# AV moved into 64x64 tiles around the scores of a later block, relu's input in two PSUM banks, and a new table of priorities

## The chip, the cores and the metric

The kernel runs on one core of a Trainium2 chip. The metric is the device time of one execution in microseconds (us). Five engines work in parallel, each with its own instruction order fixed when the program is built: TensorE (PE, with its weight loads as PEld), VectorE (DVE), ScalarE (ACT), GpSimd (POOL) and SyncE (SP), which here only issues DMAs. They wait for each other by semaphores.

## The reference

Attention within a window of 32 positions to both sides, over 8 batches, 8 heads, 576 positions and 64 channels, followed by two matrix products with a squared relu between them:

```python
scores = np.matmul(q, k.transpose(0, 1, 3, 2)) / np.sqrt(64)
scores = np.where(np.abs(pos[:, None] - pos[None, :]) <= 32, scores, -1e9)
attn = np.exp(scores - np.max(scores, axis=-1, keepdims=True))
attn = attn / (np.sum(attn, axis=-1, keepdims=True) + 1e-09)
x = np.matmul(attn, v)          # to 4608 tokens x 512
r = np.maximum(x @ w_in, 0.0)   # 512 x 2048
out = (s * (r * r) + b) @ w_out # 2048 x 512
```

Inputs and output are float32; the products run in bfloat16.

## The kernel before

The 4608 tokens are cut into 36 blocks of 128. Block `j` goes through these steps:

- SP loads q, k and v of the block (three DMAs of 256 KB, L456; in two pieces where a block crosses a batch). POOL, and early ACT and DVE, cast them to bf16 (`kqn`, `ve`, and `vo`, which is v shifted by half a block). `turned` and `lastload` keep the loads in one order on SP.
- q and k are transposed into `kqt`: by PE up to block 8, from there by one DMA transpose of 256 KB on SP (`k_turn`, L539).
- `scores` (L596): 16 matmuls on 64x64 quarters of the PE array into the two `SC` banks. Where the ring of `kqt` buffers wraps, a part of them is split and there are 24.
- DVE adds the mask and takes the maximum (L605), ACT takes the exponential with its sum (L612), DVE inverts the sum (L620, L623), POOL multiplies (L477). The result `p` is transposed into `pts`: by PE for blocks 0 to 3, then by a DMA transpose of 256 KB on SP (L639).
- `av` (L667): 16 matmuls of 128 rows by 64 columns of weights each (the page writes 128*64), into one bank `AV`. DVE casts this to `XT` (L476, the group `xt<-av`).

The rest is the feed-forward part (FFN), in 8 tiles of 128 tokens and then 14 of 256. `s1` (L758): `XT` times `w_in`, 16 matmuls of 128 columns or 8 of 256, into a PSUM bank: `HT[0]`, `HT[1]` and, from token 1024 on, also `TPF` (shown as `tp`). ACT takes the relu of the bank (L767), DVE squares it (L786). `s2` (L809): 16 matmuls of 512 columns, in steps of four, into `OUTP` or `PTPF` (shown as `ptp`), in the last three tiles also into `SC[1]` and `AV`. DVE scales and adds (L818, `outs`), SP stores 256 KB (L823). Where the plan expects PE to be idle early on, `fill` (L408) puts matmuls of no use into the order.

The order on every engine comes from a planner, `_Plan.order`. It walks through time with a cost for each step, and on each engine takes the ready step with the least `key`: about the token number, an offset for the kind of the step, and `RANK`, a shift by kind (two rows: blocks 0 to 11, and the others). For PE it adds 95 ns (`SWITCH`) when the mode of tiling changes (full array, 128*64, 64*64). For a DMA it keeps a time at which the DMA engines are free, and adds `dtime`. The order is then fixed; on the chip an engine that meets a wait stops, and what stands behind it on that engine stops too.

Of the kernel before, what the change touches and what calls it, by code (L numbers as in the profile page):

```python
# [24 lines left out]
PE_SLACK, STEADY = 400.0, 60000.0  # L25
SWITCH, STICK, STAY = 95.0, 1500, 60000.0
BIAS = {"act": 0.0, "dve": 400.0, "pool": 0.0}
FILL, FILL_MIN, FILL_SHARE, FILL_NS, WARM = ("attn", "ffn", "sums"), 300.0, 0.7, 115.0, 9000.0
# [34 lines left out]
class _Plan:  # L63
# [10 lines left out]
    def add(self, eng, fn, cost, key, reads=(), writes=(), dsem=None, ndma=1, dtime=0.0,  # L74
            after=(), behind=None, ndesc=128):
        n = _Node(len(self.nodes), eng, fn, cost, 300.0 if eng == "pe" else 130.0, key, dsem,
                  ndma, dtime)
        n.ndesc = ndesc

        def dep(m, raw):  # L80
            if m is not None and m is not n:
                n.deps[m] = bool(n.deps.get(m)) or raw

        for m in after:
            dep(m, True)
        if behind is not None:
            assert behind.eng == eng
            n.deps[behind] = None
        for r in reads:
            dep(self.writers.get(r), True)  # L90
        for w in writes:
            dep(self.writers.get(w), True)
            for m in self.readers.get(w, ()):
                dep(m, False)
        for r in reads:
            self.readers.setdefault(r, []).append(n)
        for w in writes:
            self.writers[w] = n
            self.readers[w] = []
        self.nodes.append(n)  # L100
        return n

    def order(self):
# [29 lines left out]
        while len(out) < len(self.nodes):  # L133
# [29 lines left out]
            if e == "pe" and n.mode != mode:  # L163
                free[e], mode = free[e] + SWITCH, n.mode
            if n.dsem is None:
                end = free[e] + n.lat
            else:
                early = t < STEADY
                if e == "sp" and early:
                    free[e] = room(free[e], n.ndesc)  # L170
                dma_free[e] = max(dma_free[e], free[e] + (ISSUE if early else 1300.0)) + n.dtime
                if e == "sp" and early:
                    dma_free[e] += TURN if (n.ndesc == 512) != (kind == 512) else 0.0
                    kind = n.ndesc
                end = dma_free[e] + (LAND if early else 700.0)
                if e == "sp":
                    queue.append((dma_free[e], n.dtime, n.ndesc))
                    del queue[:-12]
            for u in n.users:
                if u.deps[n] is None:  # L180
                    u.ready = max(u.ready, free[e])
                else:
                    late = PE_SLACK if u.eng == "pe" and t > STEADY else 0.0
                    u.ready = max(u.ready,
                                  end + late if u.eng != n.eng or n.dsem else free[e] + 60.0)
                u.left -= 1
                if u.left == 0:
                    offer(u)
# [70 lines left out]
    stage = None  # L259


def bass_sliding_window_symmetric__then__act_starrelu_kernel(
# [15 lines left out]
    LEAD, L0, LS = 640, 300, 50  # L278
# [13 lines left out]
    RANK = ({"ptc": 200, "ou": 120, "no": -20, "av": -120, "vo": 0, "ktc": 0, "ck": 200, "rc": -160, "cv": 20, "ktd": 320, "cq": 400, "wo": 340, "s1": -240, "kt": -60, "wi": -40, "xt": -280, "re": 80, "pt": -40}, {"vo": 40, "pt": -60, "ex": -200, "ck": -320, "s2": -80, "av": 580, "qt": -320, "mx": 320, "s1": -20, "sc": 40, "kt": 80})  # L292
    EARLY = 12

    def rank(kind, j):
        return RANK[0 if j < EARLY else 1].get(kind, 0)

# [10 lines left out]
    def OSET(j):  # L308
        return ("act", "dve")
# [3 lines left out]
    with ExitStack() as es:  # L313
# [45 lines left out]
        PTPF = ps((128, 512), F32, "ptp")  # L359
        AV = ps((128, NPAIR, 128), F32, "av")  # L360
# [91 lines left out]
        def load(src, t0, dst, name, key, sem, x):  # L452
            pcs = parts(t0)

            def fn(e):
                return [e.dma_start(dst[r:r + n, :].rearrange("p (h d) -> p h d", h=H),  # L456
                                    src[b, :, s0:s0 + n, :].rearrange("h s d -> s h d"))
                        for (b, s0, r, n) in pcs]

            tot = sum(n for (_, _, _, n) in pcs)  # L460
            gate = turned.get(x - GATE)
            lastload[0] = add("sp", fn, 640.0 * len(pcs), key, writes=[name], dsem=sem,
                              ndma=len(pcs), dtime=1150.0 * tot / 128, behind=lastload[0], ndesc=8 * tot,
                              after=[gate] if gate and gate.eng == "pe" else [])
            if gate and gate.eng == "sp":
                lastload[0].deps.setdefault(gate, None)

        def cast(engs, src, sname, dst, dname, key, costs=None):
            move(engs, costs or {"act": 620.0, "dve": 425.0, "pool": 640.0}, dst, src, key,
                 sname if isinstance(sname, list) else [sname], [dname])  # L470
# [46 lines left out]
        def make_vo(j):  # L517
# [9 lines left out]
            for r0, x in ((64, j), (0, j + 1)):  # L527
                sl = x % (NL + 1)
                move(OSET(j), {"act": 620.0, "dve": 425.0},
                     VO[s_][r0:r0 + 64, :], V32[sl][r0:r0 + 64, :],  # L530
                     akey(j) - 10 + rank("vo", j), [("V32", sl)] + ([("V32", 0, "lo")] if x == 0 else []),
                     [("VO", s_, r0)])


        def k_turn(j):
            kn, kt = j % NB, j % NKT
            key = akey(j) - 128
            if j > KQDMA:
                add("sp", lambda e: [e.dma_start_transpose(KQT[kt][:, :, :], KQN[kn][:, :])],  # L539
                    1300, key + 64 + rank("ktd", j), reads=[("KN", kn), ("QN", kn)],  # L540
                    writes=[("KT", kt), ("QT", kt)], dsem=f"dkt{kt}", dtime=1600, ndesc=1024)
                return
# [7 lines left out]
            move(FLEX(j - 1), {"dve": 430.0, "act": 620.0}, KQT[kt][:, 0:NPAIR, :], TP[:, 0:4, :],  # L550
                 key + rank("ktc", j), ["TP"], [("KT", kt)])

        def q_turn(j):
# [12 lines left out]
            move(FLEX(j), {"dve": 430.0, "act": 620.0}, KQT[qt][:, NPAIR:2 * NPAIR, :], TP[:, 4:8, :],  # L566
                 key + rank("qtc", j), ["TP"], [("QT", qt)])

        def attend(j):
# [7 lines left out]
            def half(blk, pr, a):  # L577
                return ((NKT - 1 - blk) * 2 * NPAIR + pr) * 2 + a

            def scores(e):  # L580
# [19 lines left out]
            add("pe", scores, 215, key + rank("sc", j), reads=[("KT", ka), ("KT", kb), ("QT", kb)],  # L600
                writes=[("SC", 0), ("SC", 1)]).mode = 2
            for y in range(8):
# [12 lines left out]
                    390, key + 2 + rank("ex", j), reads=[("SS", ss, x), ("MX", mb, y)],  # L615
                    writes=[("P", pb, y), ("SM", mb, y)])
            fine = j < FINE
            for c0, c1 in ((0, 4), (4, 8)) if fine else ((0, 8),):
# [5 lines left out]
                    180, key + 3 + rank("rc", j), reads=[("SE", mb, c0)] + [("SM", mb, y) for y in ys],  # L624
# [7 lines left out]
            for part, (c0, c1) in enumerate(((0, 4), (4, 8)) if fine else ((0, 8),)):  # L632
# [5 lines left out]
                if j >= PDMA:  # L638
# [3 lines left out]
                        writes=[("PTS", ptb, y) for y in range(8)], dsem=f"dpt{ptb}", dtime=1600, ndesc=1024)  # L642
                else:
                    def turn(e, c0=c0, c1=c1, ptp=ptp):
                        for y in range(c0, c1):
# [6 lines left out]
                         {"act": 190.0 + 0.83 * 128 * (c1 - c0), "dve": 50 + 95.0 * (c1 - c0)},  # L652
                         PTS[ptb][:, c0:c1, :], ptp[:, c0:c1, :], key + 4 + rank("ptc", j), [pres],
                         [("PTS", ptb, y) for y in range(c0, c1)])

                split = j < NSPLIT
# [4 lines left out]
                for step in steps:  # L661
                    def av(e, c0=c0, c1=c1, avp=avp, step=step, opens=step is steps[0],
# [11 lines left out]
                    n = add("pe", av, (28 if split else 27) * (c1 - c0), key + 5 + rank("av", j),  # L674
# [6 lines left out]
                     {"act": 190.0 + 0.83 * 64 * (c1 - c0), "dve": 150 + 68.0 * (c1 - c0)},  # L681
# [8 lines left out]
        def cvec():  # L690
            for c in range(4):
# [6 lines left out]
                add("pe", fn, 872, -300 + c + rank("cs", 0), reads=["ONES"] + [("WOUT", f) for f in range(4 * c, 4 * c + 4)],  # L698
# [38 lines left out]
        for m, nt in enumerate(TILES):  # L737
            ends = m >= len(TILES) - TAIL
            attention_until(NT if ends else max((t0 + nt) // 128, FIRST.count("|")))
# [6 lines left out]
            for f0 in range(0, 16, fg):  # L746
                hb, rb = hcnt[0] % (3 if KQDMA < NT and t0 >= 128 * KQDMA else 2), rcnt[0] % NR1
# [15 lines left out]
                add("pe", s1, 4 * fg * (2.5 + 0.4167 * nt) + 8, key + rank("s1", t0 // 128),  # L763
# [8 lines left out]
                if t0 < 128 * NWHOLE:  # L772
                    add(("act", "dve"), {"act": relu, "dve": relu_dve},
                        {"act": 600.0, "dve": 600.0}, key - RELU + rank("re", t0 // 128), reads=[hres],
                        writes=[("R1", rb)])
                else:
                    add("act", relu, 600, key - RELU + rank("re", t0 // 128), reads=[hres], writes=[("R1", rb)])
# [16 lines left out]
            for sub in range(nt // 128):  # L794
                r0 = t0 + 128 * sub
                end = r0 + 128 == T
                for c0, cn in ((0, 256), (256, 256)) if end else ((0, 512),):
                    ob = ocnt[0] % NO
                    op_, ores = ((OUTP[:, :], ("OUTP", 0)), (PTPF[:, :], "PTP"),
                                 (SC[1][:, :, :].rearrange("p a b -> p (a b)"), ("SC", 1)),  # L800
                                 (AV[:, :, :].rearrange("p a b -> p (a b)"), "AV"),
                                 )[0 if ocnt[0] < NSOLO else ocnt[0] % (4 if last else 2)]
                    ocnt[0] += 1
                    for pt in range(4):
# [9 lines left out]
                        add("pe", s2, 872 * cn / 512, key + rank("s2", t0 // 128),  # L814
# [6 lines left out]
                        60 + 1.35 * cn, key - 2000 + rank("ou", t0 // 128), reads=[ores, "CVEC", "SCB"], writes=[("OUTS", ob)])  # L821
# [63 lines left out]
```

## Time and profile before

| | us |
|---|---|
| median of three runs (323.91 to 324.71) | 323.96 |
| span of the profiled execution, first to last instruction | 322.6 |
| time outside the span (median less span) | 1.4 |
| first matmul starts / last matmul ends, from the span's start | 1.3 / 319.9 |
| TensorE clock granted, all slices | 1.00 |
| busy: PE / ACT / DVE / POOL | 309.6 / 237.1 / 219.0 / 188.1 |

The profiled execution is one; the three runs lie within 0.25% of each other. The page gives busy time by engine, the span in 40 slices (tenths of busy time), the chain of waits that ended last, and groups of equal instructions. Matmuls overlap, so what a matmul costs is read from one start to the next, in the timeline, not from its mean duration. A share of the DMA engines over 1 means that the packets on one engine overlap.

### The profile page before, as it was taken

Reading aid. Unit: us, or ns where it says so; the run is one execution under the profiler, and the core shown is the slowest. Engines: PE = TensorE matmul, PEld = TensorE weight load, DVE = VectorE, ACT = ScalarE, POOL = GpSimd, SP = SyncE. Lnnn points to the kernel's source line nnn. Section 1 sums busy time; section 2 is a strip of 40 time slices with the busy share of each in tenths; the row PEclk is TensorE's granted clock in tenths of the full one; section 3 lists DMA queues with packets and bytes.
Section 4 is the critical chain, followed back from the end, with each engine's and each line's share of the span. In section 5 each row is a group of like instructions: output and inputs, shape, how many; then the busy total and the mean of one; then the engine's idle time right before and its main releaser. Section 6 shows DMA issues by size and latency. Waiting matters only on the chain.

```text
span 322.6 us, 9452 instructions
## 1 busy us (share of the span) xinstructions
PE 309.6 (96%) x3437; PEld 210.7 (65%) x3437; DVE 219.0 (68%) x939; ACT 237.1 (73%) x804; POOL 188.1 (58%) x402
## 2 busy tenths in 40 slices
PE   6879899998999999999999999999999999999996
PEld 4557675757775766566666766676766666766664
DVE  3657848976896678787677875678776766644242
ACT  4988977896995878797578986788889888624130
POOL 1555785886878275769565887467686754420000
PEclk9999999999999999999999999999999999999999
DMA  7999999999999999999999999999999992230011
GB/s 143 293 285 267 399 262 221 213 207 216 201 215 182 257 212 178 223 212 227 214 217 219 200 197 216 216 230 188 194 234 211 240 157 67 68 98 2 33 68 65
DMA packets 185887, 62.49 MB, mean 194 GB/s; under 512 B 177008, under 2 KB 177264, under 8 KB 185840
## 3 DMA queue, kind: packets, MB, share of 16 engines
q1 hardware_dynamic: 185552, 61.88, 94.6%
q8 instruction: 27, 0.44, 0.6%
q14 instruction: 20, 0.16, 0.2%
q10 hardware_dynamic: 288, 0.00, 0.0%
HBM read 36.70 MB, written 9.44 MB: 143 GB/s over the span
## 4 chain that ended last, share of the span: by engine, by line
PE 77%; SPq 8%; DMA 8%; POOL 3%; DVE 2%; ACT 1%; issue 1%; POOLq 0%
PE ht L758 24%; PE outp L809 15%; PE ptp L809 15%; PE tp L758 10%; SPq L456 7%; PE av L667 4%; DMA q<-in_q_dram 3%; PE sc L596 3%; PE sc L809 2%; DMA kqt<-kqn 2%; POOL p L477 2%; DMA v<-in_v_dram 2%; PE av L809 2%; DMA pts<-p 1%; PE outp L694 1%; SPq L431 1%
## 5 line engine op out<-in xcount | busy, mean ns | idle before, releaser
L477 POOL TENSOR_SCALAR p<-p,rc 128x128 bf16<-128x128 bf16 x275 | 112.7, 428 | 35.9 <-DVE rc L623 35.9
L612 ACT ACTIVATE p<-ss,mx 128x128 bf16<-128x128 f32 x288 | 111.8, 391 | 11.1 <-DVE mx L605 10.6
L758 PE MATMUL ht<-xt,win 128*128 128x256 bf16 (+1 forms) x1104 | 106.5, 248 | 0.2
L786 DVE TENSOR_TENSOR gt<-r 128x512 bf16<-128x512 bf16 x144 | 71.3, 497 | 48.2 <-ACT r L767 46.3
L758 PEld LDWEIGHTS ht<-xt,win 128*128 128x128 bf16 x1104 | 86.5, 98 | 18.2 <-ACT r L767 0.6
L767 ACT ACTIVATE r<-ht 128x512 bf16<-128x512 f32 x106 | 62.4, 591 | 31.2 <-PE ht L758 29.7
L605 DVE CUSTOM_DVE_ANT_0 ss<-sc,mask 128x128 f32<-128x128 f32 x288 | 66.2, 282 | 8.8 <-PE sc L596 8.5
L809 PE MATMUL outp<-wout,gt 128*128 128x512 bf16 (+1 forms) x272 | 67.8, 373 | 0.0
L809 PE MATMUL ptp<-wout,gt 128*128 128x512 bf16 x256 | 65.5, 379 | 0.0
L612 ACT ACTIVATION_READ_ACCUMULATOR p<-ss,mx 128x1 f32 x288 | 54.6, 189 | 0.0
L758 PE MATMUL tp<-xt,win 128*128 128x256 bf16 x304 | 39.4, 273 | 0.0
L809 PEld LDWEIGHTS ptp<-wout,gt 128*128 128x128 bf16 x256 | 24.2, 98 | 22.1
L809 PEld LDWEIGHTS outp<-wout,gt 128*128 128x128 bf16 x272 | 24.9, 98 | 20.1
L476 POOL CAST ve<-v 128x512 bf16<-128x512 f32 x37 | 24.1, 651 | 24.0 <-PE av L667 14.4
L481 ACT CAST vo<-v 64x512 bf16<-64x512 f32 x45 | 27.6, 614 | 12.0 <-PE av L667 10.3
L758 PEld LDWEIGHTS tp<-xt,win 128*128 128x128 bf16 x304 | 29.3, 98 | 7.5
L476 POOL CAST kqn<-k 128x512 bf16<-128x512 f32 x33 | 21.4, 648 | 20.8 <-DMA k<-in_k_dram 20.7
L767 ACT ACTIVATE r<-tp 128x512 bf16<-128x512 f32 x38 | 22.4, 590 | 14.6 <-PE tp L758 13.3
L476 DVE CAST xt<-av 128x512 bf16<-128x512 f32 (+1 forms) x34 | 23.1, 680 | 9.0 <-PE av L667 8.8
L476 POOL CAST kqn<-q 128x512 bf16<-128x512 f32 x34 | 22.5, 661 | 10.4 <-DMA q<-in_q_dram 10.3
L605 DVE DVE_READ_ACCUMULATOR2_ANT mx<- 128x1 f32 x288 | 23.0, 80 | 0.0
L596 PEld LDWEIGHTS sc<-kqt 64*64 64x64 bf16 x632 | 9.8, 106 | 12.5 <-issue 8.5
(69 smaller groups left out, 229.7 us busy)
## 6 DMA issues: line engine op xcount, KB each, us to landing
out_dram<-outs SPq DMA_DIRECT2D x35, 256.0 KB, 2.9
q<-in_q_dram SPq DMA_DIRECT2D x32, 256.0 KB, 4.7
k<-in_k_dram SPq DMA_DIRECT2D x28, 256.0 KB, 4.5
v<-in_v_dram SPq DMA_DIRECT2D x28, 256.0 KB, 4.8
gt<-in_moe_w_in_dram SPq DMA_DIRECT2D x4, 1024.0 KB, 8.3
gt<-in_moe_w_out_dram SPq DMA_DIRECT2D x4, 1024.0 KB, 9.3
k<-in_k_dram SPq DMA_DIRECT2D x8, 192.0 KB, 3.6
v<-in_v_dram SPq DMA_DIRECT2D x8, 192.0 KB, 4.3
```

Of the source, the lines that this page charges most:

```text
L456: return [e.dma_start(dst[r:r + n, :].rearrange("p (h d) -> p h d", h=H), src[b, :, s0:s0 + n, :].rearrange("h s d -> s h d")) for (b, s0, ...
L476: return e.tensor_copy(dst, src)
L477: return e.tensor_scalar(dst, src, scale, 1.0, ALU.mult, ALU.mult)
L481: return e.copy(dst, src)
L596: r = e.matmul(dst, rhs=rhs, start=True, stop=True, lhsT=KQT[kb][r0:r0 + 64, NPAIR + pr, 64 * u:64 * u + 64])
L605: lambda e, ss=ss, x=x, y=y: e.tensor_tensor_reduce(out=SS[ss][:, x, :], in0=SC[y % 2][:, y // 2, :], in1=MASK[kind][:, :], scale=-SCALE, ...
L612: lambda e, ss=ss, x=x, y=y: e.activation(P[pb][:, y, :], SS[ss][:, x, :], AF.Exp, bias=MX[mb][:, y:y + 1], scale=-1.0, accum_out=SM[mb][: ...
L667: r = e.matmul(avp[64 * hh:64 * hh + 64, pr, 64 * u:64 * u + 64], lhsT=vt[k0:k1, 128 * pr + 64 * hh:128 * pr + 64 * hh + 64], rhs=PTS[ptb] ...
L758: r = e.matmul(hbank[:, nt * f:nt * f + nt], lhsT=WIN[:, kc, 128 * ft:128 * ft + 128], rhs=XT[:, kc, x0:x0 + nt], start=(kc == 0), stop=(k ...
L767: return e.activation(R1[rb][:, :], hbank[:, :], AF.Relu, bias=0.0, scale=1.0)
L786: return e.tensor_tensor(d, r, r, ALU.mult)
L809: r = e.matmul(op_[:, 0:cn], lhsT=GT[:, g_, fc, :], rhs=WOUT[:, fc, c0:c0 + cn], start=(fc == 0), stop=(fc == 15))
```

## The change

From block 11 on (`GRP`), the AV of block `j - 3` (`LAG`) is issued around the scores of block `j`. Each of its 16 matmuls is cut in two of 64 rows by 64 columns, so that AV runs in the same tiling as the scores: 16 matmuls (`n1`), the scores (`n2`), the other 16 matmuls (`n3`). The two halves of the 64 tokens go to two banks, `PA[:, 0]` (formerly `PTPF`) and `PA[:, 1]` (formerly `AV`), and one DVE cast reads both. `n3` waits for `n1` by a semaphore, because the two halves of the array must not write to one bank at once. AV of blocks 0 to 7 and 33 to 35 stays as it was.

`THIRD = "out"` takes `TPF` away from relu's input, which keeps two banks, and gives it to `s2` as its second bank in the place of `PTPF`. `RANK` becomes a table by kind and block (15 columns, the last for all later blocks). The planner's costs change, among them the price of a change of tiling (`TRANS`, by direction), the time from a PE step to its user, `PE_SLACK`, and `dtime` of a load (1150 to 1100 ns for 256 KB) and of a DMA transpose (1600 to 1350). `LEAD` and `LS`, which say how far attention runs ahead, become 576 and 80 (from 640 and 50). No step of the computation is added or dropped.

```diff
-PE_SLACK, STEADY = 400.0, 60000.0
-SWITCH, STICK, STAY = 95.0, 1500, 60000.0
+PE_SLACK, STEADY = 300.0, 60000.0
+STICK, STAY = 1500, 60000.0
+TRANS = {(0, 1): 93.0, (0, 2): 93.0, (1, 0): 112.0, (2, 0): 135.0, (2, 1): 132.0, (1, 2): 110.0}
+RANK = {
+    "av": (-1220, 900, -960, -860, -260, 0, -620, 1600, -10320, -10320, -10320, -10320, -10320, -10320, 420),
...
+GRP, LAG, THIRD = 11, 3, "out"
+LEAD, L0, LS = 576, 300, 80
...
-                free[e], mode = free[e] + SWITCH, n.mode
+                free[e], mode = free[e] + TRANS[mode, n.mode], n.mode
...
-    LEAD, L0, LS = 640, 300, 50
...
-        PTPF = ps((128, 512), F32, "ptp")
-        AV = ps((128, NPAIR, 128), F32, "av")
+        PA = ps((128, 2, 512), F32, "av")
+        PTPF = PA[:, 0, :]
+        AV = PA[:, 1, :].rearrange("p (a b) -> p a b", b=128)
...
-                              ndma=len(pcs), dtime=1150.0 * tot / 128, behind=lastload[0], ndesc=8 * tot,
+                              ndma=len(pcs), dtime=1100.0 * tot / 128, behind=lastload[0], ndesc=8 * tot,
...
+            def av_part(e, part):
+                for pr in range(NPAIR):
+                    for u in range(2):
+                        r0 = 64 * (u ^ part)
+                        for hh in range(2):
+                            r = e.matmul(PA[64 * hh:64 * hh + 64, u, 64 * pr:64 * pr + 64],
+                                         lhsT=vvt[u][r0:r0 + 64, 128 * pr + 64 * hh:128 * pr + 64 * hh + 64],
+                                         rhs=PTS[jv % NPT][r0:r0 + 64, 2 * pr + hh, 64 * u:64 * u + 64],
+                                         start=(part == 0 and pr == 0), stop=(part == 1 and pr == NPAIR - 1))
+                return r
...
+                n1 = add("pe", lambda e: av_part(e, 0), 128, gk, reads=vrd + krd,
+                         writes=["PTP", "AV", ("SC", 0), ("SC", 1)])
+                n2 = add("pe", scores, 223, gk - 5000, reads=krd, writes=[("SC", 0), ("SC", 1)])
+                n3 = add("pe", lambda e: av_part(e, 1), 128, gk - 5000, reads=vrd,
+                         writes=["PTP", "AV"], after=[n2])
+                n3.hard = n1
+                n1.mode = n2.mode = n3.mode = 2
+                x0 = 128 * (jv % NX)
+                move("dve", {"dve": 640.0},
+                     XT[:, :, x0:x0 + 128].rearrange("p c (u t) -> p u c t", u=2),
+                     PA[:, :, 0:256].rearrange("p u (c t) -> p u c t", t=64),
+                     key + 5 + rank("xt", j), ["PTP", "AV"], [("XT", jv % NX, 0)])
...
-                        writes=[("PTS", ptb, y) for y in range(8)], dsem=f"dpt{ptb}", dtime=1600, ndesc=1024)
+                        writes=[("PTS", ptb, y) for y in range(8)], dsem=f"dpt{ptb}", dtime=1350, ndesc=1024)
...
-                hb, rb = hcnt[0] % (3 if KQDMA < NT and t0 >= 128 * KQDMA else 2), rcnt[0] % NR1
+                hb, rb = hcnt[0] % (3 if THIRD == "ht" and t0 >= 128 * KQDMA else 2), rcnt[0] % NR1
...
+                    two = (PTPF, "PTP") if last or t0 < 128 * (GRP - LAG - 2) else (TPF[:, :], "TP")
```

## The prediction

> **What bounds the kernel now.** The page first: span, busy time, slices.
>
> ```profile
> span 322.6 us, 9452 instructions
> PE 309.6 (96%) x3437; PEld 210.7 (65%) x3437; DVE 219.0 (68%) x939; ACT 237.1 (73%) x804; POOL 188.1 (58%) x402
> PE   6879899998999999999999999999999999999996
> DMA  7999999999999999999999999999999992230011
> ```
>
> PE is full but for the first 40 us, and the DMA engines are full up to about 262 us. Two resources run side by side at their limit, and a plan that speeds up one meets the other. Next the PE timeline, where a step's price is the distance between starts:
>
> ```profile
> 144.98 1.03 PE L809 MATMUL ptp<-wout,gt 128*128 128x512 bf16 x4
> 145.93 0.42 PE L596 MATMUL sc<-kqt 64*64 64x128 bf16 x16
> 146.28 1.04 PE L809 MATMUL outp<-wout,gt 128*128 128x512 bf16 x4
> 147.25 0.32 PE L667 MATMUL av<-pts,ve 128*64 128x64 bf16 x8
> ...
> 157.20 1.03 PE L809 MATMUL outp<-wout,gt 128*128 128x512 bf16 x4
> 158.16 0.44 PE L596 MATMUL sc<-kqt 64*64 64x128 bf16 x24
> 158.53 0.32 PE L667 MATMUL av<-pts,ve 128*64 128x64 bf16 x8
> 158.68 0.29 PE L667 MATMUL av<-pts,vo 128*64 128x64 bf16 x8
> 158.91 0.83 PE L758 MATMUL ht<-xt,win 128*128 128x256 bf16 x6
> ```
>
> Four matmuls of 512 columns take 0.864 elsewhere (4 x 0.216); in front of scores or AV 0.95 to 0.96. So 0.093 is the price of entering another tiling. Taking single starts from the trace in the same way, leaving it costs 0.135 after scores, 0.117 after 64-column matmuls on 64*64, and 0.112 after AV; scores to AV costs 0.132, AV to scores 0.110. Net of that, 16 score matmuls take 0.223, 16 AV matmuls 0.256, and the 24 of split scores 0.24.
>
> With these prices the whole PE order of before adds up: 277.2 useful work, 12.3 fillers, 14.3 changes of tiling (130 of them), together 303.8. From the first matmul at 1.3 to the last end at 319.9 there are 318.6, so 14.7 is waiting: all but 2.9 of it before 38.8, and of that 2.3 in three waits for DMA transposes (AV at 71.8 and 132.4, scores at 77.6).
>
> Last the DMA side, SP's timeline and the windows (columns: window, length, busy PE, PEld, DVE, ACT, POOL, clock, DMA share, GB/s):
>
> ```profile
> 44.79 1.23 SPq L456 DMA_DIRECT2D q<-in_q_dram  x1
> ...
> 54.26 1.14 SPq L823 DMA_DIRECT2D out_dram<-outs  x1
> ```
>
> ```profile
> 87.74 1.36 SPq L539 DMA_TRANSPOSE kqt<-kqn  x1
> ...
> 113.97 3.72 SPq L539 DMA_TRANSPOSE kqt<-kqn  x1
> ```
>
> ```profile
> 65.00:90.00 25.00, 23.46 (x375) 17.22 (x374) 18.85 (x88) 20.64 (x73) 19.73 (x43) 1.00 1.29 208
> 90.00:115.00 25.00, 25.00 (x280) 16.62 (x279) 18.62 (x70) 18.61 (x63) 14.92 (x34) 1.00 1.26 225
> 120.00:165.00 45.00, 44.46 (x477) 28.97 (x476) 33.60 (x151) 34.20 (x124) 31.16 (x67) 1.00 1.09 206
> 210.00:260.00 50.00, 50.00 (x555) 33.97 (x544) 37.68 (x170) 42.85 (x150) 35.94 (x79) 1.00 1.14 210
> ```
>
> Eight loads in a row are issued from 44.79 to 54.26, each issue held up by the full queue: 1.18 per load. Between the two key transposes at 87.74 and 113.97 stand 12 loads, 7 transposes and 4 stores in 26.2, again with issues that wait. The loads take 14.2 of it; stores landed 0.64 to 0.80 behind the DMA ahead of them, say 0.7; 1.3 remains per transpose. Up to 115 the queue is saturated (share 1.26 to 1.29); later it has a little air (1.09 to 1.14). The key transposes land only 0.5 to 6 before the scores that need them, mostly 1 to 3: in steady state attention is paced by DMA with hardly any reserve.
>
> **The change, part by part.** *PE order.* The changed program holds 25 groups of AV, scores, AV. Its 400 AV matmuls have become 800 of half the rows; four of them, one per quarter, replace two. The nearest row is the split scores, whose 64-column matmuls start in pairs 0.031 apart while the other two quarters work beside them: 8 ns each, so 32 take 0.256 as before. Changes of tiling fall from 130 to 98, 14.3 to 10.9; leaving a group after 64-column matmuls saves 25 x 0.018 more, so 10.4. Useful work stays at 277.2; fillers are 104 in place of 113, 11.3. Sum 299.0, 4.8 below before.
>
> At this place a rule of the Trainium skill speaks against the change ("TensorE: Matmul & The Clock Gate", "Wait — 56ns, not 53.3ns?"): starts of matmuls are never closer than about 25 ns, however short. By it 16 more matmuls per group would cost 0.4, or 10 in 25 groups. The trace disagrees: 24 start within 0.24 at 158.16.
>
> *The new wait.* `n3` waits for `n1`, and all of PE's queue stands behind it. The last matmul of `n1` takes 0.19 from its start (row of the scores' 64x64 matmuls: 195 ns), and another engine's end reaches a waiting one 0.05 later (AV ends at 72.22, the cast starts at 72.27). The scores in between cover 0.223 of this 0.24. I take 0.02 per group, 0.5 in all; from 0 (wholly covered) to 0.24 each (nothing covered, 6.0).
>
> *Relu in two banks.* A bank must be refilled no sooner than 0.17 (rest of the last matmul) + 0.05 + 0.59 (relu, L767) + 0.05 = 0.86 after its last use, 1.24 with one exponential ahead on ACT (0.384 from start to start). By the order the least distance is 1.34, and 11 of 130 lie under 1.65 (before: 1.74, none): two exponentials ahead would stall these by 0.3. I take 0, at most 3. The cast over two banks has the same 512 elements; its row (xt, 680 ns, DVE 68% busy) hides it. `tp` in place of `ptp` for `s2` costs nothing: outputs are at least 2.5 of PE work apart, the DVE step takes 0.67.
>
> *Start-up.* Up to 38.6 casts and loads set the pace, in the same order of loads. There the old order has 278.5 left and the new one 275.7 when AV of block 2 ends; less 0.45, plus the 0.5. Without a later wait the last matmul then ends at 38.6 + 275.7 + 0.6 (small gaps, as before) = 314.9, the span is 317.6 (2.65 for the last store, as now), and the time with the 1.4 outside the span **319.0**; a landmark up to 1 earlier gives 318.
>
> *Where attention is put.* This decides. In the new order blocks 11 to 33 follow each other every 6.59 of PE work (before: 7.4 from start to start), and 77.6 of PE work is left when the group of block 33 starts (before: 61.7). So without waits this group starts at 237. It needs the `pts` transpose of block 30. Follow SP's order: up to the key transpose for block 11 the same DMAs stand ahead in both programs (41 loads, 8 weights, 4 stores, 4 + 4 transposes); in before it landed at 91.4 out of a full queue. From there to `pts` of block 30 stand 66 loads, 45 transposes and 18 stores: 77.9 + 59.0 + 12.6 = 149.5, so 240.9 at the earliest, with no idle moment. The stretch from 77.6 to 121.0 (18 loads, 13 transposes, 5 stores, priced 41.8, took 43.4) gives a factor 1.04, hence 246.9; before's pace over the same piece (162.9 for nearly the same list) gives 253. I take 244, near the saturated rows: the order asks for about 7 us more than the queue gives. PE stands in front of each group and waits, with all later FFN work behind it; this moves the end by 7.
>
> A page of the skill would price this otherwise ("DMA: Bandwidth & Descriptors", "Latency and other measured facts"): a DMA transpose moves 261 GB/s, which is an estimated 1.0 per 256 KB. The 45 would take 14 less and the wait would be gone. The rows above say 1.3.
>
> **Forecast.** 319.0 + 7 = **326.0**: slower by 0.6%. Its own range 322.5 to 329, from landings at 240.9 to 247.
>
> **Rivals.** *DMA keeps pace* (faster, 319.0; 317.5 to 321.5). For it: with other timing less of the queue may be lost between transposes and loads, and up to 254 the engines had about 9 us of air from 78 on. It decides if 22 sets (three loads, two transposes, most of a store) take 6.6 each or less; the saturated rows show 6.8 to 7.1. *Relu waits* (slower, about 330): PE 3 later on top of the 7. Against it: the distances above. *The quarters run two at a time*: 32 AV matmuls in 0.51, 25 x 0.256 = 6.4, hidden in part by the same DMA waits: 326 to 329. Against it: the scores' row. *The self-wait is not covered*: 25 x 0.22 = 5.5, likewise hidden in part: 325 to 328. That the change is not what it says is excluded: the groups stand in the order.
>
> **How the numbers follow.** About 1 us (0.3%) can be told from no change: 323.0 to 324.9 is the same. Chances: DMA sets the pace 0.55 (of this 0.03 under 323.0, 0.10 the same), DMA keeps pace 0.32 (0.02 the same), relu 0.06, two at a time 0.04, self-wait 0.03. Faster 0.32 - 0.02 + 0.03 = 0.33, same 0.12, slower 0.55. The range runs from 318.0, through most of the second case, to 329.5.
>
> **What would show it.** Right: waits of PE for `pts` or `kqt` at groups that add up to 4 to 10 from 90 to 245, group 33 at 241 to 247, a DMA share near 1.25 all that time, AV groups of 0.7 from entry to exit. Wrong: group 33 near 237 with no such waits (second case); scores to second AV half longer than 0.25 (self-wait); 64x64 AV matmuls 16 ns apart; waits of `s1` for ACT.

## The result and the profile after

The changed kernel takes 338.61 us (median of 4, 336.11 to 338.97), the kernel before 323.97 beside it: a ratio of 1.043 (1.039 to 1.047). The profiled execution took 338.48, its span is 336.7.

Its page, the same rows as before and the granted clock:

```profile
span 336.7 us, 10264 instructions
PE 313.0 (93%) x3828; PEld 214.7 (64%) x3828; DVE 216.2 (64%) x946; ACT 233.6 (69%) x798; POOL 188.4 (56%) x401
PE   6988989998979997999889999889889999999996
PEclk9799999999979998999979999999999999999999
DMA  7999999999999999999999999999999621221012
```

The holes in PE lie between slices 8 and 31, as long as the DMA row reads 9; behind that PE is full to the end. The PE timeline:

```profile
89.89 1.95 PE L827 MATMUL ht<-xt,win 128*128 128x128 bf16 x32
...
94.67 0.22 PE L621 MATMUL av<-pts,ve 64*64 64x64 bf16 x2 [1.98 <-DMA pts<-p]
...
95.64 3.15 PE L827 MATMUL ht<-xt,win 128*128 128x128 bf16 x32
...
256.57 0.22 PE L621 MATMUL av<-pts,ve 64*64 64x64 bf16 x2
...
256.72 0.40 PE L643 MATMUL sc<-kqt 64*64 64x128 bf16 x16
256.97 0.22 PE L621 MATMUL av<-pts,ve 64*64 64x64 bf16 x2
...
257.22 1.04 PE L879 MATMUL tp<-wout,gt 128*128 128x512 bf16 x4
```

At 94.67 a group stands 1.98 in front of its `pts`. Then the same 32 matmuls that took 1.95 at 89.89 take 3.15: the clock has dropped. At 256.57 the group of block 33 starts (first half of AV 0.15, scores 0.25, second half with the exit 0.25). The forecast had it at 244. It does not wait itself: the last group that waits is that of block 32, at 249.74.

PE's waits behind 45 us (in all, times, longest):

```profile
PE av L621 <- DMA pts<-p: 10.2, 9, 2.3
PE av L621 <- DMA kqt<-kqn: 2.2, 1, 2.2
PE outp L761 <- POOL wout L509: 1.4, 1, 1.4
PE sc L643 <- DMA kqt<-kqn: 0.9, 1, 0.9
```

13.3 us for DMA transposes. The kernel before has 2.0 in the same view:

```profile
PE av L667 <- DMA pts<-p: 1.2, 2, 0.7
PE sc L596 <- DMA kqt<-kqn: 0.8, 1, 0.8
```

The windows, columns as before:

```profile
65.00:90.00 25.00, 24.10 (x377) 17.45 (x376) 18.42 (x88) 21.17 (x77) 17.50 (x39) 1.00 1.22 205
90.00:115.00 25.00, 23.02 (x314) 16.79 (x312) 16.36 (x80) 20.02 (x73) 17.62 (x40) 0.93 1.20 202
120.00:165.00 45.00, 42.76 (x562) 29.79 (x561) 31.83 (x148) 36.35 (x131) 30.91 (x67) 0.96 1.19 206
210.00:260.00 50.00, 45.04 (x618) 30.27 (x616) 34.76 (x166) 37.26 (x135) 34.22 (x72) 1.00 1.19 208
```

In the last three windows PE is busy 1.7 to 5.0 us less than before, yet the DMA engines move no more: 202 to 208 GB/s in the four windows, against 206 to 225. And `pts` of block 30 lands at 255.5 in both kernels.

### The profile page after: what moved, and what is told of

Read it like the earlier page. It is cut to its first block, busy times and chain, and to the rows that moved or that the text cites. A ratio compares the mean times of both kernels' runs of the same rounds, so it can differ in the third digit from the quotient of the medians.

```text
span 336.7 us, 10264 instructions
## 1 busy us (share of the span) xinstructions
PE 313.0 (93%) x3828; PEld 214.7 (64%) x3828; DVE 216.2 (64%) x946; ACT 233.6 (69%) x798; POOL 188.4 (56%) x401
## 4 chain that ended last, share of the span: by engine, by line
PE 49%; DMA 20%; SPq 9%; POOL 8%; ACT 5%; DVE 4%; issue 4%; POOLq 0%; DVEq 0%
PE ht L827 20%; PE outp L879 10%; PE tp L879 7%; DMA q<-in_q_dram 7%; DMA pts<-p 5%; POOL p L510 4%; SPq L489 4%; DMA gt<-in_moe_w_out_dram 3%; ACT p L677 3%; PE av L879 3%; DMA k<-in_k_dram 3%; SPq L704 2%; POOL kqn L509 2%; PE sc L879 2%; SPq L572 2%
## 5 line engine op out<-in xcount | busy, mean ns | idle before, releaser
L827 PE MATMUL ht<-xt,win 128*128 128x256 bf16 (+1 forms) x1408 | 148.2, 258 | 0.3
L827 PEld LDWEIGHTS ht<-xt,win 128*128 128x128 bf16 x1408 | 118.3, 100 | 29.6 <-ACT r L836 0.4
L836 ACT ACTIVATE r<-ht 128x512 bf16<-128x512 f32 x144 | 84.6, 588 | 46.5 <-PE ht L827 41.6
L855 DVE TENSOR_TENSOR gt<-r 128x512 bf16<-128x512 bf16 x144 | 67.8, 471 | 60.5 <-ACT r L836 59.2
L879 PE MATMUL tp<-wout,gt 128*128 128x512 bf16 x192 | 48.4, 379 | 0.0
L879 PEld LDWEIGHTS tp<-wout,gt 128*128 128x128 bf16 x192 | 18.4, 98 | 14.7
L621 PE MATMUL av<-pts,ve 64*64 64x64 bf16 x400 | 15.9, 199 | 12.5 <-DMA pts<-p 10.2
L621 PEld LDWEIGHTS av<-pts,ve 64*64 64x64 bf16 x400 | 10.7, 109 | 21.7 <-issue 16.3
L879 PE MATMUL av<-wout,gt 128*128 128x512 bf16 (+1 forms) x96 | 22.0, 362 | 0.0
L643 PE MATMUL sc<-kqt 64*64 64x128 bf16 (+1 forms) x632 | 15.4, 219 | 1.4 <-DMA kqt<-kqn 0.9
```

Source lines behind the costliest of these rows:

```text
L621: r = e.matmul(PA[64 * hh:64 * hh + 64, u, 64 * pr:64 * pr + 64], lhsT=vvt[u][r0:r0 + 64, 128 * pr + 64 * hh:128 * pr + 64 * hh + 64], rhs ...
L643: r = e.matmul(dst, rhs=rhs, start=True, stop=True, lhsT=KQT[kb][r0:r0 + 64, NPAIR + pr, 64 * u:64 * u + 64])
L827: r = e.matmul(hbank[:, nt * f:nt * f + nt], lhsT=WIN[:, kc, 128 * ft:128 * ft + 128], rhs=XT[:, kc, x0:x0 + nt], start=(kc == 0), stop=(k ...
L836: return e.activation(R1[rb][:, :], hbank[:, :], AF.Relu, bias=0.0, scale=1.0)
L855: return e.tensor_tensor(d, r, r, ALU.mult)
L879: r = e.matmul(op_[:, 0:cn], lhsT=GT[:, g_, fc, :], rhs=WOUT[:, fc, c0:c0 + cn], start=(fc == 0), stop=(fc == 15))
```

## The experiments

Times are medians; ratios are to the kernel before, run beside them, with the 95% interval. "Pace" is the time from the landing of `pts` of block 11 to that of block 30, divided by 19: 7.47 in the kernel before, 7.30 in the changed one ("after"). Order sums are worked out as in the prediction.

**e1: the planner's DMA prices as before.** `dtime` in the plan, nothing else:

```diff
-  dtime=1100.0 * tot / 128   # load        -  dtime=1350   # both transposes
+  dtime=1150.0 * tot / 128                 +  dtime=1600
```

> The changed kernel with the planner's old prices for a load (1150 ns) and a DMA transpose (1600 ns); everything else is new. By its order the group of block 33 has 64.0 us of PE work behind it (changed kernel 77.6, before 61.7). Theory A, the DMA queue gives a set of three loads, two transposes and most of a store no faster than every 7.4 us, and the changed plan asks for 6.6: group 33 again at about 254 to 256, then 64 + 4 us, so 321 to 325; waits of PE for DMAs after 60 us fall from 13 to under 5. Theory B, the latency from the scores of a block to its pts (20 to 22 us in the changed kernel) is longer than three blocks of the new order: the pace of blocks is 6.8 us here, three of them 20.3, so most waits stay and the time is 330 or more. Theory C, the new priorities as such (order of casts, relu in two banks) cost the time: 335 or more.

Measured: 337.81, 1.043 (1.038 to 1.049). Wrong for A. The part that A is about did happen: between 113 and 278 PE waits 1.6 for `pts`, and never for `kqt`. But 6 us (waits, and work at half clock) are lost near 101 to 107 and about 9 between 278 and 300. Something else takes the gain when the pace fits. The number lies in the ranges of B and C; B's waits for `pts` are not there, and e4, with the same kind of priorities, speaks against C.

**e2: new priorities and prices without the groups.** `GRP, LAG, THIRD = 99, 0, "out"`.

> The changed kernel with AV left as it was before for all blocks (one step of 16 matmuls, one bank), new priorities and prices as they are. 4.4 us more for changes of tiling, pace of blocks 6.5 us by its order, 82.7 us of PE work behind the scores of block 33. Theory A: scores of block 33 near 255, end at 255 + 82.7 + 4 = 340 to 345. Theory B: AV no longer holds up the scores, so the waits for pts go: 326 to 332. Theory C: about as the changed kernel plus 4, 341 to 344.

Measured: 337.25, 1.043 (1.038 to 1.048), in none of the three ranges. Without a single group the time is the same: AV waits 5.8 for `pts` and the scores 5.6 for `kqt` behind 45 us. So the 64x64 matmuls and `n3`'s wait are not needed for the loss. The order asks for a block every 6.5 us, and its pace is 7.07. `pts` of block 30 lands at 247.5, 8 us earlier than with the groups; the time does not show it, because this order leaves 82.7 of PE work behind the scores of block 33, and not 77.6.

**e3: the groups alone.** The kernel before with the groups, the two banks of AV and relu's two banks; old priorities, prices and `LEAD`. In the plan a PE step may follow a PE step at once (before: 60 ns later), here and in the runs built on it (e6, e7, e10, e11, e13, e14, e16, e18).

> The kernel before with the grouping alone: AV in 64x64 tiles around the scores of three blocks later, two banks, one cast, relu in two banks; old priorities, old prices, old lead; a PE step that follows a PE step may follow at once in the plan (else the groups are torn apart). By its order 3.9 us less PE work than before, pace of blocks 7.1 us, 60.8 us of PE work behind group 33. Theory A: group 33 at about 255, end at 255 + 60.8 + 4 = 319.5 to 322, faster than before. Theory B: three blocks are 21.4 us, waits for pts of some 3 to 6 us: 322 to 326. Theory C, if it is the two relu banks: 326 or more.

Measured: 339.88, 1.050 (1.046 to 1.055), far above A and B. It lies in C's open range, but e10 below puts relu's two banks at under 3. The order asks for 7.14 per block, and between 113 and 278 PE waits only 1.3 for DMA. Most of the loss lies at the ends: 5.5 us between 97 and 114, and 10.7 behind 279, work at half clock included. The PE timeline there (the rows left out are the rest of the group):

```profile
287.35 3.67 PE L797 MATMUL ht<-xt,win 128*128 128x256 bf16 x32 [0.20 <-ACT r L806]
294.93 0.42 PE L704 MATMUL av<-pts,ve 128*64 128x64 bf16 x8 [3.91 <-DMA pts<-p]
295.17 0.40 PE L704 MATMUL av<-pts,vo 128*64 128x64 bf16 x8
...
296.61 0.65 PE L613 MATMUL sc<-kqt 64*64 64x128 bf16 x16
...
298.28 3.56 PE L797 MATMUL ht<-xt,win 128*128 128x256 bf16 x16 [0.81 <-DVE xt L479]
```

A single AV (L704) stands in front of scores (L613), and both are late. This is block 34's AV ahead of block 35's scores. `attend(33)` puts AV of 33 into the program, and only then `attend(34)` its group; both write the bank `AV`, so the group of 34 may not start before AV of 33, which needs `pts` of 33. There 13 us pass from the scores of a block to the landing of its `pts`, and its AV starts 13 to 17 behind its scores. So at the end attention goes scores 33, AV 33, scores 34, AV 34, scores 35, AV 35, one round trip after the other: 263.6, 279.8, 281.5, 294.9, 296.6, 313.9.

After has the same chain (256.6, 273.8, 276.2, 290.7, 293.0, 306.7). It does not wait there, since its order leaves nearly 78 us of PE work behind block 33; e1's leaves 64.0 and e3's 60.8, and the chain comes out.

**e4: lighter loads.** After, with q, k and v read as contiguous rows of 2 KB in place of eight runs of 256 B per token (so other values arrive); the order is the same.

```diff
-  src[b, :, s0:s0 + n, :].rearrange("h s d -> s h d")
+  flat[S * b + s0:S * b + s0 + n, :]
```

> The changed kernel, every instruction in its place, but q, k and v are loaded as rows of 2 KB from other places of the same tensors (not the reference's values), so that a load of 256 KB takes the DMA engines about 0.65 us, as the weights do, in place of 1.18. Theory A: a set then takes about 5.8 us, under the plan's 6.6; the waits after 60 us and the clock drops behind them go, group 33 at 237 to 239, end at 318.5 to 321. Theory B: only the landing gets about 1.5 us shorter, so half of the waits stay: 324 to 330. Theory C: 334 or more.

Measured: 317.83, 0.982 (0.978 to 0.987). Page and one window:

```profile
span 315.7 us, 10264 instructions
DMA packets 89122, 62.54 MB, mean 198 GB/s; under 512 B 66416, under 2 KB 66672, under 8 KB 89072
```

```profile
120.00:165.00 45.00, 45.00 (x641) 32.41 (x640) 35.81 (x171) 41.18 (x149) 34.07 (x74) 1.00 1.11 235
```

Same bytes, under half the packets, and PE waits for no DMA behind 45 us. The pace is 6.57, what the order asks for (6.59). The group of 33 starts at 235.7 (the prediction without waits: 237), and the time is 1.2 below the predicted 319.0 (and 0.7 below A's range). This is the run that decides: with the very same instructions on PE, the time hangs on how long the loads take. It does not say whether the queue itself was full or whether the engines that use the loads stood waiting for them: lighter loads help both.

**e5: the same loads in the kernel before.**

> The kernel before with its q, k and v loads in rows of 2 KB (contiguous, other values than the reference's; the order is that of before). It is the control of e4. Theory A (the DMA queue's pace is what the changed order runs into; before asks for 7.4 us of PE work per block and so fits it): before loses only 2.3 us in three DMA waits late, so it gains 2 to 4 us: 319.5 to 322, and stays slower than e4 (317.8) by about the 4.8 us of PE order less what start-up differs. Theory D (lighter loads help both kernels alike, by some other way than waits): about 20 us less than before, 303 to 308, which the sum of PE work (318.6 less waits) makes impossible unless waits that I read as start-up go too.

Measured: 321.54, 0.993 (0.990 to 0.995). The control holds: before gains 1.6 us (2 to 4 were expected), after 20. With light loads the change is worth 3.7 us (321.54 less 317.83), of the 4.8 that the order saves.

**e6 and e7: e3 with the chain at the end cut, then with groups from block 15.**

```diff
+  def solo(): ...            # AV of one block, as before
+  if j >= NT - LAG: late.append(solo)
+  else: solo()
...
+  if j == NT - 1:
+      for f in late: f()
```

```diff
-GRP, LAG, THIRD = 11, 3, "out"
+GRP, LAG, THIRD = 15, 3, "out"      # e7 only
```

> e3 (before with the grouping, the two banks and the old priorities) with one more edit: AV of blocks 33 to 35, which stand alone, are put into the program behind block 35 and not between the groups of 33, 34 and 35. In e3 the bank that they write chains them: scores 33 at 263.6, AV 33 at 279.8, scores 34 at 281.5, AV 34 at 294.9, scores 35 at 296.5, AV 35 at 313.9; 10.6 us of PE's waiting lies there (1.17, 0.91, 4.94, 1.00, 0.90 and 1.65 at half clock). Theory T (this chain is what eats the gain of the new order when the pace fits the DMA): scores 34 and 35 come 7 us apart, those waits go, 329 to 331. Theory U (the late transposes come late whatever the order, because the DMA queue is behind): AV 33 waits for pts as before, 336 to 340.

> e6 with the grouping from block 15 on and not from block 11 (GRP = 15). In e3 5.8 us of waiting lie between 97 and 113: AV of block 9 can only go with the scores of block 12, whose key transpose lands at 103.7, and PE has no other work; before has AV 9 at 100.8 and the scores of 12 at 107.4. Theory T: with both edits only the 3.5 us of DMA waits that e3 has at 69, 73.5 and 146.5 remain, PE's order is 299.9 against 303.8: 321 to 324. If the waiting at 97 to 113 comes from the DMA queue being behind at that time in any order, 326 to 330.

Measured: e6 327.61, 1.013 (1.011 to 1.016), 1.4 better than T's range; e7 325.76, 1.007 (1.005 to 1.010), between T and its rival. T holds for the end: scores 34 and 35 follow 33 by 7.7 each, the waits there are gone, and the time falls by 12.3. The later start of e7 empties the stretch from 97 to 114 (0.1 is left), but the time falls by 1.9 only. What remains in e7 is new: 2.7 for `pts` and 1.3 for `kqt` in front of groups. A group waits for the later of two transposes, where the kernel before let scores and AV go one by one.

**e8: both edits and the old DMA prices in after** (e1 with `late` and `GRP = 15`).

> After with the old DMA prices in the plan (as e1), AV of 33 to 35 behind block 35, and grouping from block 15 on. e1 lost 6 to 7 us at its first group (100.9, with 2.1 at half clock) and about 10 at 281 to 299, and nearly nothing between. Theory T: both go, 320 to 324. Rival U: as e1, 335 to 338; if only one place is mended, 327 to 331.

Measured: 328.76, 1.016 (1.012 to 1.020), T's case of one place mended. The end is mended; some 6.5 us between 100 and 112 remain (PE waits for the maximum, for `pts`, for `xt`, then runs at half clock), so the first block of the groups was not their cause.

**e9: one block more of distance.** `GRP, LAG = 12, 4`, one more buffer each of `ve`, `vo`, `pts`, and `late` as in e6.

> After with AV four blocks behind the scores and not three (LAG = 4, groups from block 12), one more buffer each for v, shifted v and pts, and the single AVs of 32 to 35 behind block 35. It tells a full DMA queue from a loop of latency. In after each group needs pts of three blocks before, and from the scores to the landing of pts 19 to 23 us pass, so a block can't take less than a third of that; measured, from pts of block 11 to pts of block 30, after takes 7.30 per block, e2 (the same DMAs without the groups) 7.07. Theory A (the DMA queue alone): 7.3 per block as in after, pts 30 at 254 to 257. Theory L (the loop over three blocks adds to a queue that could do 7.07): four blocks make room, 7.0 to 7.1 per block, pts 30 at 246 to 250, and PE's waits for pts go over into waits for kqt. By the new order 85 us of PE work are left behind the group of 33, so the time does not fall: L 335 to 339, A 341 to 345.

Measured: 345.2, 1.061 (1.057 to 1.066). PE's waits behind 45 us:

```profile
PE av L623 <- DMA kqt<-kqn: 13.5, 10, 2.6
...
PE av L623 <- DMA pts<-p: 3.7, 1, 3.7
```

The waits go over to `kqt`, as L expected, but blocks do not follow each other faster: 7.66, with `pts` of 30 at 262.3. The profiled execution took 350.2, 5 us more than the median; even with all of that taken off the 19 blocks the pace is 7.4. So the loop over three blocks is not the limit, and L falls. The time is at A's upper end; A's landing (254 to 257) is missed.

**e12: a fifth load buffer.** `NL, AHEAD, GATE = 5, 5, 6`, and `k5 q4 v5` at the end of the first loads.

> After with a fifth buffer for q, k and v each and the loads one block further ahead (NL 5, AHEAD 5, GATE 6). Theory A (throughput of the DMA queue): pts 11 to pts 30 as in after, 7.2 to 7.4 us per block; since the plan, which believes in the earlier loads, now leaves 82 us of PE work behind the group of 33, the time is 338 to 343. Rival R (the loop of load, POOL's cast and SP's order, with too few loads in flight): 7.0 per block or less, pts 30 at 246 to 249, 330 to 335.

Measured: 345.14, 1.066 (1.064 to 1.069), waits behind 45 us:

```profile
PE av L621 <- DMA pts<-p: 18.0, 13, 3.9
```

Pace 7.23, as A has it, `pts` 30 at 258.5, and the time 2 above A's range. The loads of k from block 20 on do land 1 to 4 us sooner than in after, but the transposes do not: more loads in flight buy nothing. With e4 and e9 this is consistent with a limit in the DMA queue's throughput for this mix, but it does not prove it, since e2 shows that nearly the same DMAs in another order can go at 7.07. One rival was not tried. In after, between 113 and 250 us, POOL stands in front of its casts of k and q until their loads land, and SP stands for POOL before it can issue a transpose of `p`:

```profile
POOL kqn L509 <- DMA k<-in_k_dram: 16.0, 10, 3.2
POOL kqn L509 <- DMA q<-in_q_dram: 11.6, 8, 3.4
```

```profile
SPq L704 <- POOL kqn L509: 11.4, 12, 1.4
```

While POOL waits for a load, what stands behind it on POOL waits too, and so do the loads behind a transpose for which SP waits. In the same stretch these waits of POOL for loads, 27.6 in after, add up to 12.6 in e2, 29.4 in e12 and 1.1 in e4. So the pace can come from the queue, or from this chain over POOL and SP; no run changes POOL's order alone, and this stays open.

**e10, e11, e13, e14: relu's bank, and groups for fewer blocks.** e10 is the kernel before with relu in two banks and no groups (and the plan's 0 ns between PE steps). e11 is e7 with `GRP = 21`. e13 and e14 are e11 and e7 with `THIRD = "ht"`: relu has three banks again, `s2` one.

> Before with relu's input in two PSUM banks only (tp taken away and left unused in steady state) and with PE to PE dependences at 0 ns in the plan; nothing else. It prices that part by itself. My prediction's value: 0, at most 3 us (323 to 326). Rival (ACT becomes late with two banks): waits of s1 for ACT, 326 to 330.

> e7 with the grouping from block 21 on (GRP = 21): 15 groups in place of 21. e7 waits 4.5 us at 134 to 168 for pts or kqt, where a group waits for the later of two transposes and the kernel before, whose AV and scores stand apart, waited 0.6; later only 1.1. Theory T: before keeps its order up to 165, where DMA still has no reserve, and each of 15 groups then saves 0.2: 320.5 to 323, faster than before by 0.3 to 1%. Rival: the groups wait for the later transpose wherever they begin: 324 to 327.

> e11 with relu's input in three banks as before and s2's outputs in one bank (THIRD = ht). e10 put the loss of relu's third bank, with another order, at 1.0051 (1.0012 to 1.0089), and e11 with 15 groups on top at 1.0076: no gain from the groups. If the bank is what eats it: 320.5 to 323 at the speed of before of 323.2 (ratio 0.992 to 0.999). Rival: s2 in one bank waits for the DVE step between outputs (0.67 us each time two outputs follow each other), ratio 1.01 or more; or the groups wait for the later of two transposes as in e11, ratio 1.004 to 1.01.

> The same with groups from block 15 on, 21 of them (e7 with three relu banks). e7 stood at 1.0071 (1.0045 to 1.0097). If the relu bank is what costs: 0.993 to 1.000. If the waits of the groups for the later transpose cost (4.5 us at 134 to 168 in e7): 1.004 to 1.01.

Measured: e10 1.005 (1.001 to 1.009), e11 1.008 (1.004 to 1.011), e13 1.002 (1.000 to 1.005), e14 1.004 (1.001 to 1.006); that is about 1.7, 2.5, 0.7 and 1.2 us, and e13 can't be told from no change. e10 lies within the 0 to 3 of the prediction, e11 and e14 are with their rivals, and e13 lies between both. Giving relu its bank back gains (e11 to e13 0.5%, e7 to e14 0.3%). But e10's trace has no wait for ACT behind 60 us; it has this:

```profile
PE sc L613 <- DMA kqt<-kqn: 4.2, 6, 1.5
```

The loss comes as DMA waits of an order that fits the queue less well, not as the waits of `s1` that my rival expected. Why the bank shifts the order so was not tried, nor the 0 ns without the bank. The 15 or 21 groups at best make up for what they cost.

**e16, e17, e18: less lead.** `LEAD` 576 in e14, 576 in the kernel before, 520 in e14.

> e14 with LEAD 576 in place of 640: attention is asked for later, 60.5 us of PE work are left behind the group of 33 in the order in place of 64. Theory A: the DMA's landings set when the last groups can start and the work behind them is 3.5 us less, so the time falls by 1 to 3 against e14 (324.6): ratio to before 0.993 to 0.999. Rival (FFN now waits for AV, which comes three blocks behind the scores): waits of s1 for xt, 1.005 or more.

> The kernel before with LEAD 576. Its order waits only 2.8 us behind 45 us, so there is little to gain: ratio 0.995 to 1.002; if FFN runs out of AV, 1.005 or more.

> e14 with LEAD 520: 57.1 us of PE work behind the group of 33. Theory A: the DMA waits go wholly, but AV comes three blocks behind the scores and FFN takes two blocks at a time, so 520 tokens (four blocks) are too few: waits of s1 for xt, ratio 1.000 to 1.015. If FFN never waits: 0.987 to 0.995.

Measured: 1.005 (1.003 to 1.008), 1.007 (1.004 to 1.009), 1.018 (1.016 to 1.021). All three lie in or above the slower range that was given. A is missed in e16: behind 45 us the waits for DMA fall from 2.7 to 1.0, but waits of `s1` for `xt` come in (2.0). With 520 tokens there are 2.6 of these, and the waits for DMA do not go (3.1), as A had said they would. Apart from e4 and e5, which read other values, no version here beats the kernel before.

## Why the prediction was wrong, step by step

**Right: the mechanism.** The order asks for blocks faster than the transposes land, PE stands in front of groups, and the end moves with the landings (e4 against e5). The waits at groups behind 90 us add up to 12.4, more than the 4 to 10 that I had named as a sign.

**Right: what lies behind.** From the group of 33 to the end of the execution I had 77.6 + 2.65 + 1.4 and small gaps, 82; measured 338.48 - 256.57 = 81.9. And without DMA waits I had 319.0; e4 took 317.8. Some luck is in this: e4's lighter loads also shorten the start (the scores of block 4 start at 49.0, in after at 50.8).

**Right: the price of the 64x64 matmuls and of the new wait.** AV halves and scores take 0.15 and 0.25 in the timeline, within 0.03 of my prices.

**Wrong: the landing of `pts` of block 30.** The step is "I take 244, near the saturated rows". `pts` of block 30 landed at 255.5 and the group started at 256.57, 12.6 later than taken; the whole time missed by 12.6, so this one term is the miss. It has three parts. The key transpose for block 11 landed at 93.6, not at before's 91.4 (2.2). The piece of 66 loads, 45 transposes and 18 stores, priced at 149.5 and taken at 152.6, took 162.0 (9.4). And the group started 1.0 behind the landing, since it follows the group of 32, which had waited for `pts` of block 29 until 249.6, in the order of PE.

My 1.18 and 1.3 came from a row of eight loads and from one saturated stretch of 26 us. Over the whole piece the changed kernel did little better than the kernel before, where it takes 164.1, with three more stores, and ends at 255.5 too. Something like that stood in the prediction, as "162.9" and "253", though 91.4 + 162.9 is 254.3; with 254.3 the sum is 336. The step that failed is thus the size of this term: the sum of single prices has no room for the moments in which POOL waits for loads and SP for POOL (11.4 us of SP's time alone in the view above). How much of the 9.4 is that, and how much a queue that is slower for the mix, is not shown; in e2 the same piece, one transpose and one store shorter, took 155.6.

**Wrong: the meaning of "air".** I read the lower DMA share of before (1.09 to 1.14) as reserve that a faster order would use. After fills it to 1.19 and moves no more bytes per second; the share near 1.25 that I had named as a sign did not come.

**Wrong: the range.** Its upper end came from a factor 1.04 over a stretch of 43 us, while the same paragraph held 253 from the whole piece. The bound that I had worked out myself was left out.

**Not seen: the chain at the end.** The prediction read the groups, but not what the order in which they enter the program does to AV of 33 to 35. In after 78 us of PE work hide it; where the order asks less of the DMA it comes out, and costs e3 12.3 us (e6) and e1 about 9. The rest of what e1 loses, 6 us near 101 to 107, is not explained.

**The rivals.** Two quarters at a time and the uncovered self-wait are excluded by the timeline. *Relu waits* did not come, within the 0 to 3 given (e10: 1.7 in all, 0.4 to 2.9). *DMA keeps pace* needed 6.6 per block: it came about only with light loads.

## What to carry to other kernels

Price a shared queue by its pace over a long stretch of the same mix, not by its best local rows, and set that against the pace that the new order asks for. A sum of single prices leaves out the waits of the engines that feed the queue. A change that saves work on PE gives nothing while something else sets the pace, and it costs when the work moved up has to wait in order on the busy engine. When two steps are joined, look at what each waited for (the pair waits for the later), and at the last few items that fall outside the joined form: a shared bank can make them serial.

## What the runs showed of the hardware

**The clock of PE is set in fixed windows of 3.41 us, and a wait of some 2 us is enough to halve it, when it falls into one of them.** In every trace with more than one drop they lie on a grid of that width. In after, the windows in which PE was busy 42%, 34% and 32% of the time (from 91.3, 128.9 and 166.4) were followed by one at half clock each; the next lowest, 66%, was not. In eight traces, behind 45 us and starting from full clock, all eleven windows under 41% were followed by half clock, and none above 50%; in between both occur. In the three windows at half clock PE was busy throughout, 10.2 us, which is an estimated 5.1 us of work lost (the 32 matmuls of 1.95 took 3.15). In after groups waited for DMA behind them, up to 249.74, so most of that should be hidden; no run shows how much. The Trainium skill ("TensorE: Matmul & The Clock Gate", "What's actually happening") has a free-running window of 3413 ns, and half clock after an idle one; the grid agrees, but here no window had to be idle.

**Packets of 256 B cost the loads more than their bytes.** With rows of 2 KB (e4) the window from 120 to 165 moved 235 GB/s, and PE's order set the pace; with 256 B (after) it moved 206, and PE waited. The Trainium skill ("DMA: Bandwidth & Descriptors", Specifications) asks for transfers of at least 512 B for the full rate; e4 agrees with it as far as 256 B and 2 KB go, and no run here tries a size between.
